# Computing the skip term of ten tiles on VectorE instead of TensorE in a state-space and gated feed-forward kernel

## The chip, the cores and the metric

The kernel runs on one core of one Trainium2 chip. The metric is the device time of one execution in microseconds. Every run named below was correct against the reference and in the fast state, with a mean granted TensorE clock of 0.996 or more of full speed in its profile. "Span" is the length of one profiled execution; it is about 1.8 us shorter than the time of the same execution.

## The reference, cut to what matters

```python
def _A_ref(x, Lambda_re, ..., Dskip):            # x: 1 x 2048 x 512
    ...                                          # h[t] = Lam_bar * h[t-1] + Bu[t]
    y = 2.0 * einsum("blp,dp->bld", hseq, Cmat).real + x * Dskip[None, None, :]
    return y

def _B_ref(x, w_gate, w_up, w_down):             # F = 1376
    return (_gelu(x @ w_gate) * (x @ w_up)) @ w_down

xn = _layernorm(x)
s = _A_ref(xn, ...)
g = _silu(_B_ref(xn, ...))
return x + s * g
```

The change concerns one term, `xn * Dskip`, an elementwise product.

## The kernel before

The 2048 rows are worked in four slabs of 512, each of four tiles of 128 rows by 512 columns. For each slab TensorE does eleven gate steps (gate and up products, four matmuls each), then the input projection of the next slab (u), then four down projections (f) of eleven products. VectorE does the recurrence: rotations by cosine and sine, a scan, rotation back, which leaves the hidden state `hst`. The y tiles of a slab are placed among the gate steps of the next slab. The skip term is four more matmuls per tile, with diagonal matrices that hold Dskip, in the same accumulation as y:

```python
Y_AT = (5, 7, 9, 10)          # gate steps of the next slab after which the y tiles stand

def y_mm(s, m, hst):
    ...
    for h in range(2):
        flush(("h", s, h))    # issue all VectorE work up to the state of this slab
    y_ps = psum.tile([P, D], FP32, name="y_ps", tag="ps")
    for j in range(2 * NPT):                       # 8 products with C
        nc.tensor.matmul(y_ps[:, :], lhsT=hst[...], rhs=C2[...], start=(j == 0), stop=False)
    for kt in range(KT):                           # 4 skip products
        nc.tensor.matmul(y_ps[:, kt * P : (kt + 1) * P], lhsT=xnT[...], rhs=diagI[:, kt, :],
                         start=False, stop=(kt == KT - 1))
    pe_takes(2 * NPT + 1)
    return y_ps

def epi(s, m, y_ps, g2):                           # end of a tile
    yg = work.tile([P, D], BF16, name="yg", tag="yg")        # two buffers each
    ot = work.tile([P, D], BF16, name="ot", tag="ot")
    def f():
        TT(out=yg[:], in0=y_ps[:, :], in1=g2[:], op=ALU.mult)
        TT(out=ot[:], in0=yg[:], in1=x_tok[:, s * M + m, :], op=ALU.add)
    dve(now() + 0.3, 0.95, f)
    nc.sync.dma_start(out=out_td[mg : mg + P, :], in_=ot[:])

def ln_out(s, m):                                  # normalised input, one slab ahead
    xn = work.tile([P, D], BF16, name="xn", tag="xn", bufs=4)
    ACT(out=xn[:], in_=x_tok[:, s * M + m, :], func=AF.Identity, ...)
    nc.sync.dma_start_transpose(out=xnT[...], in_=xn[:])
```

The order of VectorE's instructions is fixed when the kernel is built, by a small model of time. `later` queues the recurrence; `dve(ready, cost, f)` places an instruction that should be ready at a time counted in TensorE's progress, after the queued pieces that fit in before it:

```python
def drain(t, late):
    while waiting and max(clk["dve"], waiting[0][0]) + waiting[0][1] <= t + late:
        pop()                 # put the next queued piece here

def dve(ready, cost, f, late=0.8):
    drain(ready, late)
    clk["dve"] = max(clk["dve"], ready) + cost
    f()
```

On the chip nothing moves any more: an instruction whose operand is late holds up everything behind it (below, the rotation stands 1.04 us behind a late z).

Of the kernel before, what the change touches and what calls it, by code (L numbers as in the profile page):

```python
# [11 lines left out]
ALU = mybir.AluOpType  # L12
FP32 = mybir.dt.float32
BF16 = mybir.dt.bfloat16
# [5 lines left out]
def kernel(  # L20
# [17 lines left out]
    nc = tc.nc  # L38
    P = 128
    S = 2048  # L40
    D = 512
    F = 1376
    KT = D // P
    NPT = 4
    H2 = NPT // 2
    TS = 512
    NS = S // TS
# [8 lines left out]
    TT = nc.vector.tensor_tensor  # L56
# [7 lines left out]
    consts = ctx.enter_context(tc.tile_pool(name="consts", bufs=1))  # L64
    work = ctx.enter_context(tc.tile_pool(name="work", bufs=2))
# [9 lines left out]
    wd = consts.tile([P, NFT, D], BF16, name="wd")  # L75
    BT = consts.tile([P, 2, KT, D], BF16, name="BT")
    C2 = consts.tile([P, 2, NPT, D], BF16, name="C2")
    pv = consts.tile([16, P], BF16, name="pv")
    at0 = work.tile([P, NFT, TS], BF16, name="at", tag="at")
    hst0 = work.tile([P, 2, NPT, TS], BF16, name="hst", tag="hst")  # L80
# [13 lines left out]
    def load_gu(i):  # L94
        a, b = CUTS[i], CUTS[i + 1]
        nc.sync.dma_start(out=wg[:, :, a:b], in_=wg_r[:, :, a:b])  # L96
        nc.sync.dma_start(out=wu[:, :, a:b], in_=wu_r[:, :, a:b])

    def load_x(s):
        nc.sync.dma_start(out=x_tok[:, s * M : (s + 1) * M, :], in_=x_r[:, s * M : (s + 1) * M, :])  # L100
# [7 lines left out]
    load_x(1)  # L108
    load_gu(1)
    load_x(2)  # L110
    for h in range(2):
        for ri, src in enumerate((A_B_re, A_B_im)):
            for pt in (h * H2, h * H2 + 1):
                nc.sync.dma_start_transpose(
                    out=BT[:, ri, :, pt * P : (pt + 1) * P], in_=src[pt * P : (pt + 1) * P, :]
                )
    load_gu(2)


    warm = consts.tile([P, TS], BF16, name="warm")  # L120
    nc.vector.memset(warm[:], 0.0)
    halfpi = consts.tile([P, 1], FP32, name="halfpi")
    nc.vector.memset(halfpi[:], math.pi / 2)
# [182 lines left out]
        GS(out=ncre[:], in0=cre[:], scalar1=-1.0, scalar2=None, op0=ALU.mult)  # L306

    def fold_c(pt):
        tA = work.tile([P, D], FP32, name="tA", tag="tA")
        tB = work.tile([P, D], FP32, name="tB", tag="tB")  # L310
        ACT(out=tA[:], in_=CT[:, 1, pt, :], func=AF.Copy, scale=cim[:, pt : pt + 1])
        ACT(out=tB[:], in_=CT[:, 0, pt, :], func=AF.Copy, scale=cim[:, pt : pt + 1])
        dve(now() + 0.8, 0.66, lambda: STT(
            out=C2[:, 0, pt, :], in0=CT[:, 0, pt, :], scalar=cre[:, pt : pt + 1], in1=tA[:],
            op0=ALU.mult, op1=ALU.subtract,
        ))
        dve(now() + 1.6, 0.66, lambda: STT(
            out=C2[:, 1, pt, :], in0=CT[:, 1, pt, :], scalar=ncre[:, pt : pt + 1], in1=tB[:],
            op0=ALU.mult, op1=ALU.subtract,
        ))  # L320
# [6 lines left out]
    def now():  # L327
        return clk["pe"]

    def pe_takes(n, one=0.2157):  # L330
        clk["pe"] += n * one
# [6 lines left out]
    def flush(key):  # L338
        while any(w[3] == key for w in waiting):
            pop()  # L340

    def drain(t, late):
        while waiting and max(clk["dve"], waiting[0][0]) + waiting[0][1] <= t + late:
            pop()
# [5 lines that stand above are left out]
# [5 lines left out]
    ini = {}  # L355
    U_BUFS = 3
    U0_AT = (5, 7)
    Y_AT = (5, 7, 9, 10)

    def ca_wide():  # L360
        ACT(out=v4(ca[:]), in_=ch[:, :, NB : NB + NA].unsqueeze(3).to_broadcast(W4), func=AF.Copy)
# [107 lines left out]
    def down(s, m, at):  # L469
        m0 = m * P  # L470
        f_ps = psum.tile([P, D], FP32, name="f_ps", tag="ps")
        for k in range(NFT):
            fs = min(P, F - k * P)
            nc.tensor.matmul(  # L474
                f_ps[:, :], lhsT=at[:fs, k, m0 : m0 + P], rhs=wd[:fs, k, :], start=(k == 0), stop=(k == NFT - 1)
            )
        pe_takes(NFT)
        g2 = work.tile([P, D], FP32, name="g2", tag="g2", bufs=6)
        ACT(out=g2[:], in_=f_ps[:, :], func=AF.Silu)  # L479
        return g2  # L480

    def y_mm(s, m, hst):
        m0 = m * P
        mg = s * TS + m0
        for h in range(2):
            flush(("h", s, h))
        y_ps = psum.tile([P, D], FP32, name="y_ps", tag="ps")
        for j in range(2 * NPT):
            nc.tensor.matmul(  # L489
                y_ps[:, :], lhsT=hst[:, j // NPT, j % NPT, m0 : m0 + P], rhs=C2[:, j // NPT, j % NPT, :],  # L490
                start=(j == 0), stop=False,
            )
        for kt in range(KT):
            nc.tensor.matmul(  # L494
                y_ps[:, kt * P : (kt + 1) * P], lhsT=xnT[:, kt, mg : mg + P], rhs=diagI[:, kt, :],
                start=False, stop=(kt == KT - 1),
            )
        pe_takes(2 * NPT + 1)
        return y_ps

    def epi(s, m, y_ps, g2):
        mg = s * TS + m * P
        yg = work.tile([P, D], BF16, name="yg", tag="yg")
        ot = work.tile([P, D], BF16, name="ot", tag="ot")

        def f():
            TT(out=yg[:], in0=y_ps[:, :], in1=g2[:], op=ALU.mult)  # L507
            TT(out=ot[:], in0=yg[:], in1=x_tok[:, s * M + m, :], op=ALU.add)

        dve(now() + 0.3, 0.95, f)  # L510
        nc.sync.dma_start(out=out_td[mg : mg + P, :], in_=ot[:])

    def y_halves(s, m, hst, g2):
# [4 lines left out]
        for i in range(2):  # L518
            c = slice(i * D // 2, (i + 1) * D // 2)
            y_ps = psum.tile([P, D // 2], FP32, name="y_ps", tag="ps")  # L520
            for j in range(2 * NPT):
                nc.tensor.matmul(  # L522
                    y_ps[:, :], lhsT=hst[:, j // NPT, j % NPT, m0 : m0 + P], rhs=C2[:, j // NPT, j % NPT, c],
                    start=(j == 0), stop=False,
# [22 lines left out]
    def ln_small(s):  # L547
# [9 lines left out]
        nc.gpsimd.tensor_tensor(out=rs[:, s, :], in0=var, in1=mhalf[:], op=ALU.pow)  # L557
        nc.gpsimd.tensor_tensor(out=nb[:, s, :], in0=nm[:, s, :], in1=rs[:, s, :], op=ALU.mult)

    def ln_out(s, m):  # L560
        xn = work.tile([P, D], BF16, name="xn", tag="xn", bufs=4)
        ACT(out=xn[:], in_=x_tok[:, s * M + m, :], func=AF.Identity, scale=rs[:, s, m : m + 1], bias=nb[:, s, m : m + 1])  # L562
        c0 = s * TS + m * P
        nc.sync.dma_start_transpose(out=xnT[:, :, c0 : c0 + P], in_=xn[:])


    clk["pe"] = 8.1
    clk["dve"] = 10.3
    hsts, ats, g2s = {0: hst0}, {0: at0}, {}
# [10 lines left out]
    def ln_vector_small(x):  # L580
        G.tensor_scalar(out=vx[:, x, :], in0=mv[:, x, :, 1], scalar1=EPS, scalar2=None, op0=ALU.add)
        G.tensor_tensor(out=rs[:, x, :], in0=vx[:, x, :], in1=mhalf[:], op=ALU.pow)
        G.tensor_tensor(out=nb[:, x, :], in0=mv[:, x, :, 0], in1=rs[:, x, :], op=ALU.mult)
        G.tensor_scalar(out=nb[:, x, :], in0=nb[:, x, :], scalar1=-1.0, scalar2=None, op0=ALU.mult)
# [12 lines left out]
    for s in range(NS):  # L597
        for j in range(NFT):
            ffn(s, j, ats[s])
            if s == 0:  # L600
                if j == 1:
                    ca_wide()
                    coefficients()
                if j == 3:
                    ln_vector_small(2)
                if j == 8:
                    coefficients_end()
                if 3 <= j < 3 + M:
                    ln_out(1, j - 3)
                if j == 2 + M:  # L610
                    load_c(0)
                    nc.sync.dma_start(
                        out=wd[:, 0 : NFT - 1, :],
                        in_=B_w_down[0 : (NFT - 1) * P, :].rearrange("(k p) d -> p k d", p=P),
                    )
                    nc.sync.dma_start(out=wd[:FL, NFT - 1, :], in_=B_w_down[(NFT - 1) * P : F, :])
                    load_c(1)
                    load_x(3)
                if j in U0_AT:
                    chain(0, U0_AT.index(j), u_pair(0, U0_AT.index(j)), hst0)  # L620
            else:
                if s < NS - 1 and 1 <= j < 1 + M:
                    ln_out(s + 1, j - 1)
                if j in Y_AT:
                    m = Y_AT.index(j)
                    epi(s - 1, m, y_mm(s - 1, m, hsts[s - 1]), g2s[s - 1, m])
        if s < NS - 1:
            hsts[s + 1] = work.tile([P, 2, NPT, TS], BF16, name="hst", tag="hst")
            ats[s + 1] = work.tile([P, NFT, TS], BF16, name="at", tag="at")
            for h in range(2):  # L630
                chain(s + 1, h, u_pair(s + 1, h), hsts[s + 1])
            for m in range(M):
                g2s[s, m] = down(s, m, ats[s])
                if s == 0:
                    fold_c(m)
                    skip_diag(m)
                if s == 1:
                    ln_act(3, m)
            if s == 1:
                ln_small(3)  # L640
    s = NS - 1
# [38 lines left out]
```

## Time and profile before

The kernel took 186.52 us (median of 3, 186.51 to 186.91) before the prediction was made.

| of the span of 184.9 us | busy us | share |
|---|---|---|
| TensorE matmuls (PE) | 178.8 | 97% |
| VectorE (DVE) | 154.3 | 83% |
| ScalarE (ACT) | 111.9 | 61% |
| GpSimd (POOL) | 20.6 | 11% |

A share is an average over stages. To weigh this change three more views are needed. The groups by shape price one instruction. TensorE's timeline gives the distance between starts, because matmuls overlap (a product with C lasts 379 ns on average, but they start 216 ns apart), so that their durations cannot be added. VectorE's timeline tells when each slab's state is complete, to be set against the moment when TensorE asks for it. The prediction shows these lines.

### The profile page before, as it was taken

The page shows a single profiled execution, that of the slowest core. Times are in us where ns is not written, and L with a number is a line of the kernel's source. Part 1 is how long each engine was busy: PE and PEld are TensorE (multiplying, and loading weights), DVE is VectorE, ACT ScalarE, POOL GpSimd, SP SyncE. Part 2 cuts the span into 40 slices and gives each one's busy share as a digit, 9 for nine tenths or more (in the row PEclk, how much of TensorE's full clock was granted, in tenths as well). Part 3 has the DMA queues.
Part 4 walks back from the last instruction along what each step waited for, and adds up shares of the span by engine and source line. Part 5 has one row for each costly group of instructions (what it writes and reads, how often), then busy time and mean ns, then how long its engine had stood idle before and what let it go on. Part 6 is the DMA issues. An engine that isn't in the chain of part 4 may idle for free.

```text
span 184.9 us, 2493 instructions
## 1 busy us (share of the span) xinstructions
PE 178.8 (97%) x887; PEld 86.0 (46%) x903; DVE 154.3 (83%) x238; ACT 111.9 (61%) x196; POOL 20.6 (11%) x44
## 2 busy tenths in 40 slices
PE   7899999999999999999999999999999999999992
PEld 2474444544444444544444444544444444554452
DVE  4978999999999999999999999989999993332034
ACT  3199997768999745267889954347339643441210
POOL 3677503600000000000004000000000000000000
PEclk9999999999999999999999999999999999999999
DMA  5999694793001400000000420100000000010001
GB/s 144 309 361 128 102 239 100 212 245 109 0 0 28 85 32 28 28 28 0 0 4 5 80 57 2 34 28 28 0 0 0 4 0 28 28 37 25 28 28 57
DMA packets 24444, 12.26 MB, mean 66 GB/s; under 512 B 15760, under 2 KB 24432, under 8 KB 24432
## 3 DMA queue, kind: packets, MB, share of 16 engines
q1 hardware_dynamic: 24256, 12.03, 27.0%
q8 instruction: 7, 0.11, 0.3%
q10 hardware_dynamic: 176, 0.07, 0.1%
q14 instruction: 5, 0.04, 0.1%
HBM read 6.33 MB, written 2.10 MB: 46 GB/s over the span
## 4 chain that ended last, share of the span: by engine, by line
PE 93%; DMA 3%; SPq 1%; issue 1%; DVE 0%
PE up_ps L228 21%; PE f_ps L474 20%; PE g_ps L228 20%; PE u_ps L373 15%; PE y_ps L489 14%; DMA wu<-in_B_w_up_dram 3%; PE y_ps L494 2%; PE y_ps L522 1%; SPq L89 1%; SPq L96 0%; PE tp L175 0%; DVE yg L532 0%; DVE ot L533 0%; PE y_ps L528 0%
## 5 line engine op out<-in xcount | busy, mean ns | idle before, releaser
L228 PE MATMUL up_ps<-xnT,wu 128*128 128x512 bf16 (+2 forms) x181 | 45.2, 370 | 0.6 <-DMA wu<-in_B_w_up_dram 0.3
L228 PE MATMUL g_ps<-xnT,wg 128*128 128x512 bf16 (+2 forms) x179 | 44.9, 369 | 0.6 <-ACT xnT L196 0.5
L461 ACT ACTIVATE gt<-g_ps 128x512 bf16<-128x512 f32 (+1 forms) x44 | 27.1, 616 | 20.4 <-PE g_ps L228 16.9
L474 PE MATMUL f_ps<-wd,at 128*128 128x512 bf16 (+1 forms) x172 | 38.5, 379 | 0.2
L462 ACT ACTIVATE ub<-up_ps 128x512 bf16<-128x512 f32 (+1 forms) x44 | 27.3, 620 | 6.7 <-PE up_ps L228 6.4
L419 DVE TENSOR_TENSOR_SCAN Ft<-rho,it,Wt 128x512 bf16<-128x512 f32 x24 | 29.2, 1266 | 0.0
L373 PE MATMUL u_ps<-xnT,BT 128*128 128x512 bf16 x127 | 28.4, 379 | 0.1
L489 PE MATMUL y_ps<-C,hst 128*128 128x512 bf16 x117 | 28.2, 379 | 0.2
L228 PEld LDWEIGHTS <-wu 128*128 128x128 bf16 (+1 forms) x184 | 18.3, 100 | 20.2 <-DMA wu<-in_B_w_up_dram 0.6
L474 PEld LDWEIGHTS <-at 128*128 128x128 bf16 (+1 forms) x176 | 17.1, 98 | 20.6
L228 PEld LDWEIGHTS <-wg 128*128 128x128 bf16 (+1 forms) x184 | 17.9, 100 | 18.1 <-DMA wg<-in_B_w_gate_dram 0.6
L378 ACT ACTIVATE U<-u_ps 128x512 bf16<-128x512 f32 x32 | 19.0, 615 | 10.8 <-PE u_ps L373 10.7
L507 DVE TENSOR_TENSOR yg<-y_ps,g 128x512 bf16<-128x512 f32 x15 | 10.3, 685 | 14.1 <-PE y_ps L494 10.3
L479 ACT ACTIVATE g<-f_ps 128x512 f32<-128x512 f32 x16 | 9.6, 598 | 18.5 <-PE f_ps L474 18.5
L373 PEld LDWEIGHTS <-BT 128*128 128x128 bf16 x128 | 12.5, 98 | 14.6
L489 PEld LDWEIGHTS <-hst 128*128 128x128 bf16 x120 | 11.7, 98 | 13.6
L467 DVE TENSOR_TENSOR at<-gt,ub 128x1024 bf16<-128x1024 bf16 x20 | 13.6, 680 | 5.0 <-ACT ub L462 5.0
L393 DVE TENSOR_TENSOR hst<-pp,qq 128x1024 bf16<-128x1024 bf16 x16 | 10.7, 686 | 0.2
L389 DVE TENSOR_TENSOR pp<-U,cos_b 128x2048 bf16<-128x2048 bf16 x8 | 9.8, 1225 | 1.2 <-ACT U L378 0.8
L155 DVE BATCH_NORM_STATS2 st<-x_tok 128x6 f32<-128x512 bf16 x12 | 7.6, 682 | 3.6 <-DMA x_tok<-in_A_x_dram 3.6
L393 DVE TENSOR_TENSOR Wt<-pp,qq 128x1024 bf16<-128x1024 bf16 x16 | 10.3, 687 | 0.2
L562 ACT ACTIVATE xn<-x_tok,nb,rs 128x512 bf16<-128x512 bf16 x12 | 10.5, 874 | 0.0
(106 smaller groups left out, 148.6 us busy)
## 6 DMA issues: line engine op xcount, KB each, us to landing
out_dram<-ot SPq DMA_DIRECT2D x15, 128.0 KB, 1.7
x_tok<-in_A_x_dram SPq DMA_DIRECT2D x3, 512.0 KB, 5.4
wd<-in_B_w_down_dram SPq DMA_DIRECT2D x1, 1280.0 KB, 6.6
wg<-in_B_w_gate_dram SPq DMA_DIRECT2D x1, 640.0 KB
wu<-in_B_w_up_dram SPq DMA_DIRECT2D x1, 640.0 KB, 9.0
wg<-in_B_w_gate_dram SPq DMA_DIRECT2D x1, 384.0 KB, 5.2
wu<-in_B_w_up_dram SPq DMA_DIRECT2D x1, 384.0 KB
wg<-in_B_w_gate_dram SPq DMA_DIRECT2D x1, 352.0 KB, 3.6
```

What stands on the lines that cost most here:

```text
L228: nc.tensor.matmul(ps[:fs, a:b], lhsT=w[:, kt, fsl], rhs=xnT[:, kt, s * TS + a : s * TS + b], start=(kt == 0), stop=(kt == KT - 1),)
L373: nc.tensor.matmul(u_ps[:, :], lhsT=BT[:, ri, kt, pt * P : (pt + 1) * P], rhs=xnT[:, kt, cols], start=(kt == 0), stop=(kt == KT - 1),)
L378: ACT(out=U[:, ri, q, :], in_=u_ps[:, :], func=AF.Copy)
L393: return lambda: TT(out=dst()[i], in0=box["pp"][:, i, :, :], in1=box["qq"][:, 1 - i, :, :], op=op)
L419: nc.vector.tensor_tensor_scan(out=box["F"][:, ri, q, :], data0=rho[:, pt : pt + 1].to_broadcast([P, TS]), data1=box["W"][:, ri, q, :], in ...
L461: ACT(out=gt[:fs, i, :], in_=g_ps[:fs, :], func=AF.Gelu_apprx_tanh)
L462: ACT(out=ub[:fs, i, :], in_=u_ps[:fs, :], func=AF.Copy)
L467: dve(now() + lag, 0.61, lambda: TT(out=at[:, j - 1 : j + 1, :], in0=gt[:], in1=ub[:], op=ALU.mult))
L474: nc.tensor.matmul(f_ps[:, :], lhsT=at[:fs, k, m0 : m0 + P], rhs=wd[:fs, k, :], start=(k == 0), stop=(k == NFT - 1))
L489: nc.tensor.matmul(y_ps[:, :], lhsT=hst[:, j // NPT, j % NPT, m0 : m0 + P], rhs=C2[:, j // NPT, j % NPT, :], start=(j == 0), stop=False,)
L507: TT(out=yg[:], in0=y_ps[:, :], in1=g2[:], op=ALU.mult)
L562: ACT(out=xn[:], in_=x_tok[:, s * M + m, :], func=AF.Identity, scale=rs[:, s, m : m + 1], bias=nb[:, s, m : m + 1])
```

## The change

The intent is to take work off the engine that sets the end. For the four tiles of slabs 1 and 2 and the first two of slab 3, VectorE multiplies xn by Dskip (loaded once, broadcast over the partitions, as `Db`) as soon as xn is made. It keeps the product `z` in one of nine buffers until y of that tile is there, and adds it in fp32. Those tiles lose their four skip products. y of slab 1 moves to gate steps 1 to 4 of slab 2 (counted from 0), and y of slab 2 to steps 2, 4, 6 and 8 of slab 3. Room for z comes from shared scratch buffers.

```diff
+    Db = consts.tile([P, D], BF16, name="Db")
 ...
     load_x(2)
+    nc.sync.dma_start(out=Db[:], in_=A_Dskip.unsqueeze(0).to_broadcast([P, D]))
 ...
-    warm = consts.tile([P, TS], BF16, name="warm")
+    warm = work.tile([P, TS], BF16, name="warm", tag="yg")
 ...                                   # tA, tB: tag "tt", bufs=3, shared with yt; g2: bufs 6 -> 4
-    Y_AT = (5, 7, 9, 10)
+    Y_AT = {1: (5, 7, 9, 10), 2: (1, 2, 3, 4), 3: (2, 4, 6, 8)}
 ...
-                start=(j == 0), stop=False,
+                start=(j == 0), stop=((s, m) in zs and j == 2 * NPT - 1),
-        for kt in range(KT):
+        for kt in range(0 if (s, m) in zs else KT):
 ...
-        pe_takes(2 * NPT + 1)
+        pe_takes(2 * NPT + ((s, m) not in zs))
 ...
-            TT(out=yg[:], in0=y_ps[:, :], in1=g2[:], op=ALU.mult)
+            y = y_ps
+            if (s, m) in zs:
+                y = work.tile([P, D], FP32, name="yt", tag="tt", bufs=3)
+                TT(out=y[:], in0=y_ps[:, :], in1=zs[s, m][:], op=ALU.add)
+            TT(out=yg[:], in0=y[:, :], in1=g2[:], op=ALU.mult)
 ...
-        dve(now() + 0.3, 0.95, f)
+        dve(now() + 0.3, 1.6 if (s, m) in zs else 0.95, f)
 ...
+    def skip(s, m, xn):
+        zs[s, m] = work.tile([P, D], BF16, name="z", tag="z", bufs=9)
+        dve(now() + 1.5, 0.34, lambda: TT(out=zs[s, m][:], in0=xn[:], in1=Db[:], op=ALU.mult))
 ...                                   # in ln_out
+        if s < NS - 1 or m < 2:
+            skip(s, m, xn)
 ...                                   # in the main loop: y of a step now comes before ln_out
```

More of the change, by code (lines that the diff above doesn't have):

```diff
@@ L308, in fold_c @@
     def fold_c(pt):
-        tA = work.tile([P, D], FP32, name="tA", tag="tA")
-        tB = work.tile([P, D], FP32, name="tB", tag="tB")
+        tA = work.tile([P, D], FP32, name="tA", tag="tt", bufs=3)
+        tB = work.tile([P, D], FP32, name="tB", tag="tt", bufs=3)
         ACT(out=tA[:], in_=CT[:, 1, pt, :], func=AF.Copy, scale=cim[:, pt : pt + 1])
@@ L477, in down @@
         pe_takes(NFT)
-        g2 = work.tile([P, D], FP32, name="g2", tag="g2", bufs=6)
+        g2 = work.tile([P, D], FP32, name="g2", tag="g2", bufs=4)
         ACT(out=g2[:], in_=f_ps[:, :], func=AF.Silu)
@@ L558, in ln_small @@
         nc.gpsimd.tensor_tensor(out=nb[:, s, :], in0=nm[:, s, :], in1=rs[:, s, :], op=ALU.mult)
+    zs = {}
+    def skip(s, m, xn):
+        zs[s, m] = work.tile([P, D], BF16, name="z", tag="z", bufs=9)
+        dve(now() + 1.5, 0.34, lambda: TT(out=zs[s, m][:], in0=xn[:], in1=Db[:], op=ALU.mult))
     def ln_out(s, m):
@@ L621 @@
             else:
+                if j in Y_AT[s]:
+                    m = Y_AT[s].index(j)
+                    epi(s - 1, m, y_mm(s - 1, m, hsts[s - 1]), g2s[s - 1, m])
                 if s < NS - 1 and 1 <= j < 1 + M:
                     ln_out(s + 1, j - 1)
-                if j in Y_AT:
-                    m = Y_AT.index(j)
-                    epi(s - 1, m, y_mm(s - 1, m, hsts[s - 1]), g2s[s - 1, m])
         if s < NS - 1:
```

## The prediction

> **What bounds the kernel now.** I read the page first for who is busy and whose chain ended last.
>
> ```profile
> PE 178.8 (97%) x887; PEld 86.0 (46%) x903; DVE 154.3 (83%) x238; ACT 111.9 (61%) x196; POOL 20.6 (11%) x44
> ...
> PE   7899999999999999999999999999999999999992
> ...
> DVE  4978999999999999999999999989999993332034
> ...
> PE 93%; DMA 3%; SPq 1%; issue 1%; DVE 0%
> ```
>
> TensorE (PE) fills every slice after the start and carries 93% of the chain of work that ended last. VectorE (DVE) is just as full up to about slice 34 of 40 (157 us) and slack only after that. So TensorE sets the end now, but VectorE has nearly no idle time in which to take over work; what saves it is how far ahead of its deadlines it runs. The change moves work from the first to the second, so I need prices and deadlines. The prices are in the groups of instructions, shapes kept apart:
>
> ```profile
> L489 PE MATMUL y_ps<-C,hst 128*128 128x512 bf16 x117 | 28.2, 379 | 0.2
> ...
> L507 DVE TENSOR_TENSOR yg<-y_ps,g 128x512 bf16<-128x512 f32 x15 | 10.3, 685 | 14.1 <-PE y_ps L494 10.3 <-ACT g L479 3.8
> ...
> L508 DVE TENSOR_TENSOR ot<-yg,x_tok 128x512 bf16<-128x512 bf16 x15 | 6.4, 425 | 0.5
> ...
> L494 PE MATMUL y_ps<-diagI,xnT 128*128 128x128 bf16 x60 | 5.8, 219 | 0.0
> ```
>
> The matmul means of 379 and 219 ns overlap each other; what a matmul costs is the distance between starts, which the timeline of TensorE gives around the first y tile of slab 0:
>
> ```profile
> 61.27 1.89 PE L489 MATMUL y_ps<-C,hst 128*128 128x512 bf16 x8
> 63.00 0.39 PE L494 MATMUL y_ps<-diagI,xnT 128*128 128x128 bf16 x4
> 63.22 1.03 PE L228 MATMUL g_ps<-xnT,wg 128*128 128x512 bf16 x4
> ```
>
> Eight products with C take 1.73 us (216 ns each), the four skip products 63.22 - 63.00 = 0.22 us (about 56 ns each). After 9 us that timeline shows no idle entry at all. The deadlines on VectorE's side are the ends of the hidden state, in its timeline:
>
> ```profile
> 57.23 1.28 DVE L393 TENSOR_TENSOR hst<-pp,qq 128x1024 bf16<-128x1024 bf16 x2
> ...
> 150.55 0.68 DVE L393 TENSOR_TENSOR hst<-pp,qq 128x1024 bf16<-128x1024 bf16 x1
> 151.15 0.68 DVE L507 TENSOR_TENSOR yg<-y_ps,g 128x512 bf16<-128x512 f32 x1
> ```
>
> State of slab 0 is complete at 58.5 and its y begins at 61.27: 2.8 us of lead. State of slab 3 is complete at 151.2 and its y begins at 164.13: 12.9 us. For slabs 1 and 2 the same timelines give 91.1 against 104.48 and 123.3 against 147.70.
>
> **What the Trainium skill says.** "TensorE: Matmul & The Clock Gate", under "Wait — 56ns, not 53.3ns?", puts a warm matmul at N / 2.4 GHz plus about 2.5 ns, 55.6 ns for N = 128 and 215.7 ns for N = 512; the distances above (56 and 216) agree. "VectorE: DVE Perf Modes", section "The perf-mode tier table", gives tensor_tensor twice the rate for bf16 in SBUF and the single rate for fp32 or any PSUM operand; 425 against 685 ns agrees. So the product of xn and Db costs about 0.42 us, and an addition out of PSUM into fp32 about 0.69; the multiplication that follows reads two fp32 tiles in SBUF and stays at 0.69. "PSUM — Partial Sum Buffer", section "Engine vs sequencer instructions", says that the VectorE queue is strictly first in, first out and that matmuls start and complete in program order. The timelines agree in that a late operand holds up whatever stands behind it (the stop at 59.97 below). This makes the order of instructions decisive, so I compared the built instruction streams of both kernels, engine by engine.
>
> **The change part by part.**
>
> *Removed on TensorE.* Ten tiles (four of slab 1, four of slab 2, two of slab 3) lose 4 products each: 10 x 0.223 us = 2.23 us, all on the path that sets the end.
>
> *Added on VectorE.* Pitches, start to start, from its timeline: 0.34 us for a bf16 product that nothing behind it waits for (69.84 to 70.18 for ot), 0.72 for an operation out of PSUM whose result the next one reads (69.12 to 69.84). Ten products and ten additions: 10 x (0.34 + 0.72) = 10.6 us, taking VectorE from 154.3 busy to about 154.3 + 10 x (0.425 + 0.685) = 165.4, or 90% of the span. It costs the kernel nothing unless a deadline is missed, so I walk the new VectorE order and compare it with TensorE.
>
> *Deadline 1, y of slab 0 (61.27).* Ahead of the last state operation of slab 0 the new order has the four z of slab 1 (4 x 0.34 = 1.36), three z of slab 2 (1.02) and one more gate product (0.60). Worse, the second z of slab 2 stands behind an xn that ScalarE (ACT) only finishes at 58.96:
>
> ```profile
> 56.45 0.83 ACT L562 ACTIVATE xn<-x_tok,nb,rs 128x512 bf16<-128x512 bf16 x1
> ...
> 58.11 0.85 ACT L562 ACTIVATE xn<-x_tok,nb,rs 128x512 bf16<-128x512 bf16 x1
> ```
>
> The walk: first half of the back rotation at 54.29 + 1.36 = 55.65 (+0.05 for the fourth z, which just meets its xn); gate product 56.8; first z 57.4; the second would be due at 57.75 and waits until 59.0, 1.3 us of idling; second half of the rotation 59.36; first state operation 60.6; gate product 61.2; third z 61.8; last state operation 62.16 to 62.85 instead of 58.5. TensorE waits for it only at the seventh of the eight products (the built stream has that wait on its weight load), due at 61.27 + 6 x 0.2157 = 62.56. With 0.1 us for the load it starts near 63.0: **a new stop of about 0.45 us**.
>
> *Deadline 2, y of slab 1, brought forward to the second gate step of slab 2.* Due about 94.1 + 0.45 + 2 x 1.73 = 98.0. Its state moves from 91.1 to about 94.5 (7 or 8 z, the 1.3 us, less VectorE's 0.4 us of idle time there): 3.4 us to spare. Placing y early matters for buffers: z has nine, and the tenth product needs the first freed.
>
> *Deadline 3, y of slab 3.* From the last state operation of slab 0 (offset 62.16 - 57.84 = 4.32) to that of slab 3 VectorE gets three more z (1.02), seven additions (7 x 0.72 = 5.04), three more y tiles of slab 2 ahead of it because their steps move from 5, 7, 9, 10 to 2, 4, 6, 8 (3 x 1.06 = 3.18), and it loses 1.21 us of old idle time; one gate product comes in (0.60) and one was counted already (0.60). It starts at 150.55 + 4.32 + 1.02 + 5.04 + 3.18 - 1.21 = 162.9 and ends at 163.6. TensorE reaches y of slab 3 at 164.13 - 8 x 0.223 + 0.45 = 162.8 and needs the last piece at the seventh product, 164.1. It just holds. Behind it stand the last y of slab 2 (1.78), then the two last gate products, done near 166.0 and 166.4; the down projection asks for them at 162.8 + 16 x 0.2157 = 166.2 and at 166.7. That holds by 0.2 to 0.3 us, and my sum over 100 us of VectorE is no better than about 0.5 us: I charge 0.15 us on average.
>
> *Beside other work.* The load of Db takes one more slot of the sync queue (about 0.5 us, as the slots around it) and 128 KB. The weights wd are the closest thing behind it: issued at 32.7, landed 6.6 us later at 39.3, needed at 41.40. Hidden. The shared scratch of three buffers and g2 with four: each reuse is met by more than 0.5 us in the walk. In slabs 2 and 3 a PSUM bank that holds y comes round again eight tiles later; the tightest, third y of slab 2, frees at about 159.6 for a gate tile at 161. At the very end, the second tile of slab 3 now takes VectorE 1.78 us and the next arrives 1.95 us later, so the tail stays as it is.
>
> *Sum:* 186.52 - 2.23 + 0.45 + 0.15 = 184.9 us.
>
> **Rivals.** (1) *Full gain, 184.3.* Speaks for it: VectorE is off the chain (0%) and no TensorE idle time follows 9 us. Against: it counts shares and not deadlines; the lead of 2.8 us at slab 0 is less than the delay worked out. (2) *VectorE becomes the bound in slab 3.* Were it 2 us later than summed, the whole delay would fall on y of slab 3 and the down projection: about 186.5, no gain, or a loss beyond that. For: it has no idle time between about 17 and 152 us. Against: the costs are measured in this trace and old idle time is absorbed. (3) *The extra load delays the first slab*, a stop of 0.5 to 1 us near 19 us (B weights) or 41 us (wd): about 185.7. Against: wd has 2.1 us of slack in the queue. (4) *Slower by over 2%* would need some 6 us of new stops; only ScalarE held back by gate buffers that VectorE frees late would chain like that, and the walk leaves at least 4 us there.
>
> **Range and chances.** The floor is the full gain, 184.3, less a tenth for noise; the top allows about 1.2 us more in stops than I sum: 184.2 to 186.1. Faster by over 2% would need 182.8, 1.5 us below what removing the products can give: 0.01. Within 2%: 0.96. Slower: 0.03.
>
> **What would show it right or wrong.** The groups should show 20 skip products at the full-width line instead of 60, ten z near 0.42, ten yt near 0.69, and yg still near 0.69. TensorE's timeline should have one stop of 0.3 to 0.6 us inside the first y of slab 0, released by the state operation, with VectorE idle before the second z of slab 2; y of slab 1 without a wait; state of slab 3 complete near 163.6 with at most some tenths of waiting around 163 to 167. I am wrong if VectorE shows no idle time at that z, if TensorE waits over 1 us in slab 3, or if it waits on a transfer before 45 us.

## The result and the profile after

| | median us | range | runs |
|---|---|---|---|
| before | 186.66 | 186.51 to 186.91 | 4 |
| changed | 184.96 | 184.40 to 185.17 | 4 |

The ratio is 0.9903, with a 95% interval of 0.9877 to 0.9929. A ratio is the mean time of one kernel's fast runs over the mean of the other's in the same rounds, so it is not quite the ratio of the medians quoted beside it. The gain is about 1%. All outputs are right.

First the page of the changed kernel: busy shares, slices of the span, and the chain that ended last by engine and by line.

```profile
PE 177.8 (97%) x863; PEld 83.7 (46%) x863; DVE 163.5 (89%) x258; ACT 112.8 (62%) x196; POOL 19.9 (11%) x44
...
DVE  4886999999997999999999999999999999996053
...
PE 87%; DMA 4%; DVE 4%; ACT 2%; SPq 1%; issue 0%; DVEq 0%
PE f_ps L476 21%; PE up_ps L230 19%; PE g_ps L230 19%; PE u_ps L375 15%; PE y_ps L491 13%; DMA wu<-in_B_w_up_dram 3%; DMA out_dram<-ot 1%; ACT gt L463 1%; ACT ub L464 1%; ACT xn L575 1%; DVE hst L395 1%; SPq L90 1%; DVE qq L391 1%; PE y_ps L496 0%; DVE z L571 0%; DVE yg L513 0%
```

TensorE's row of slices reads exactly as before. VectorE is now full up to slice 36 instead of 33, and its busy time rose by 9.2 us. The chain is the most telling line. TensorE had 93% of it and has 87%, and a small group is new: ScalarE's gt, ub and xn, VectorE's z, qq and hst, and a store of ot. These are pieces of the two waits found below.

The groups, shapes kept apart (line, engine, operation, output and inputs, count | busy us, mean ns | idle before):

```profile
L513 DVE TENSOR_TENSOR yg<-yt,g 128x512 bf16<-128x512 f32 x10 | 6.9, 693 | 1.4 <-ACT g L481 1.0
L512 DVE TENSOR_TENSOR yt<-y_ps,z 128x512 f32<-128x512 f32 x10 | 6.8, 680 | 7.1 <-PE y_ps L491 7.1
...
L571 DVE TENSOR_TENSOR z<-xn,Db 128x512 bf16<-128x512 bf16 x10 | 4.1, 418 | 1.0 <-ACT xn L575 1.0
...
L496 PE MATMUL y_ps<-diagI,xnT 128*128 128x128 bf16 x20 | 1.9, 219 | 0.0
```

There are 20 skip products at this width instead of 60, ten additions and ten products. Only one z had to wait, for 1.04 us. TensorE's timeline (start, duration, engine, line, operation, count) shows where that went, in y of slab 0, slab 1 and slab 3:

```profile
61.43 2.21 PE L491 MATMUL y_ps<-C,hst 128*128 128x512 bf16 x8
63.47 0.39 PE L496 MATMUL y_ps<-diagI,xnT 128*128 128x128 bf16 x4
...
98.05 1.89 PE L491 MATMUL y_ps<-C,hst 128*128 128x512 bf16 x8
99.78 1.03 PE L230 MATMUL g_ps<-xnT,wg 128*128 128x512 bf16 x4
...
162.82 1.89 PE L491 MATMUL y_ps<-C,hst 128*128 128x512 bf16 x8
164.55 1.67 PE L476 MATMUL f_ps<-wd,at 128*128 128x512 bf16 x7
```

Read the distance from the start of the C products to the next entry. It is 1.73 us without a stop, as in slabs 1 and 3. In slab 0 it is 63.47 - 61.43 = 2.04 us, a stop of 0.31 us that prints no idle note, because it lies within a row. The tile of slab 1 goes straight on to a gate product.

VectorE's timeline says why, and what slab 3 looks like:

```profile
57.69 0.42 DVE L571 TENSOR_TENSOR z<-xn,Db 128x512 bf16<-128x512 bf16 x1
59.15 0.42 DVE L571 TENSOR_TENSOR z<-xn,Db 128x512 bf16<-128x512 bf16 x1 [1.04 <-ACT xn L575]
59.49 1.22 DVE L391 TENSOR_TENSOR qq<-Ft,sin_b 128x2048 bf16<-128x2048 bf16 x1
...
62.29 0.69 DVE L395 TENSOR_TENSOR hst<-pp,qq 128x1024 bf16<-128x1024 bf16 x1
...
162.11 1.29 DVE L395 TENSOR_TENSOR hst<-pp,qq 128x1024 bf16<-128x1024 bf16 x2
...
165.10 0.69 DVE L469 TENSOR_TENSOR at<-gt,ub 128x1024 bf16<-128x1024 bf16 x1
165.70 0.42 DVE L467 TENSOR_TENSOR at<-gt,ub 96x512 bf16<-96x512 bf16 x1
```

Behind the second z of slab 2 stand the second half of the rotation (qq) and the last two state operations of slab 0. The very last one, which the seventh C product needs, ends at 62.98. The seventh C product was due at 61.43 + 6 x 0.2157 = 62.72 and started two products before 63.47, at 63.04. In slab 3 the state is complete at 163.40, and the last gate products end at 165.79 and 166.12; no product waits for them.

A last difference is at the end. These are the last operations of VectorE, first before, then changed:

```profile
181.66 0.42 DVE L532 TENSOR_TENSOR yg<-y_ps,g 128x256 bf16<-128x256 f32 x1
182.12 0.29 DVE L533 TENSOR_TENSOR ot<-yg,x_tok 128x256 bf16<-128x256 bf16 x1
```

```profile
179.95 0.29 DVE L539 TENSOR_TENSOR ot<-yg,x_tok 128x256 bf16<-128x256 bf16 x1 [0.46 <-DMA out_dram<-ot]
180.16 0.42 DVE L538 TENSOR_TENSOR yg<-y_ps,g 128x256 bf16<-128x256 f32 x1
180.61 0.29 DVE L539 TENSOR_TENSOR ot<-yg,x_tok 128x256 bf16<-128x256 bf16 x1
```

TensorE's last matmul ended at 181.63 before and at 179.87 in the changed kernel. The rest took 182.41 - 181.63 = 0.78 us before and 180.90 - 179.87 = 1.03 us after, because the first half of the last tile waited for the store of the tile two before it, which still held one of the two ot buffers.

The two spans are thus accounted for:

| term | us | from |
|---|---|---|
| 40 skip products gone | -2.23 | 10 x 0.223 |
| stop in the first y of slab 0 | +0.31 | 2.04 - 1.73 |
| TensorE reaches that y later | +0.16 | 61.43 - 61.27 |
| tail | +0.25 | 1.03 - 0.78 |
| sum | -1.51 | spans: 183.4 - 184.9 = -1.5 |

The term of 0.16 us is there from the start: the first gate product began at 7.49 us before and at 7.70 here. In the seven other profiles of the changed kernel and its close variants (all below that leave GpSimd and slab 3 as they are, and the one with twelve tiles) it lies between 7.41 and 8.13 us. So I take it as scatter of the start. There is only one profile of the kernel before, so whether the change also moves the mean start stays open.

### The profile page after: what moved, and what is told of

Its sections match the earlier page's. It is cut to its first block, busy times and chain, and to the rows that moved or that the text cites. A ratio compares the mean times of both kernels' runs of the same rounds, so it can differ in the third digit from the quotient of the medians.

```text
span 183.4 us, 2452 instructions
## 1 busy us (share of the span) xinstructions
PE 177.8 (97%) x863; PEld 83.7 (46%) x863; DVE 163.5 (89%) x258; ACT 112.8 (62%) x196; POOL 19.9 (11%) x44
## 4 chain that ended last, share of the span: by engine, by line
PE 87%; DMA 4%; DVE 4%; ACT 2%; SPq 1%; issue 0%; DVEq 0%
PE f_ps L476 21%; PE up_ps L230 19%; PE g_ps L230 19%; PE u_ps L375 15%; PE y_ps L491 13%; DMA wu<-in_B_w_up_dram 3%; DMA out_dram<-ot 1%; ACT gt L463 1%; ACT ub L464 1%; ACT xn L575 1%; DVE hst L395 1%; SPq L90 1%; DVE qq L391 1%; PE y_ps L496 0%; DVE z L571 0%; DVE yg L513 0%
## 5 line engine op out<-in xcount | busy, mean ns | idle before, releaser
L230 PE MATMUL g_ps<-xnT,wg 128*128 128x512 bf16 (+2 forms) x184 | 45.6, 370 | 0.5 <-ACT xnT L198 0.5
L512 DVE TENSOR_TENSOR yt<-y_ps,z 128x512 f32<-128x512 f32 x10 | 6.8, 680 | 7.1 <-PE y_ps L491 7.1
L395 DVE TENSOR_TENSOR hst<-pp,qq 128x1024 bf16<-128x1024 bf16 x16 | 10.6, 687 | 0.2
```

What stands on the lines that cost most here:

```text
L230: nc.tensor.matmul(ps[:fs, a:b], lhsT=w[:, kt, fsl], rhs=xnT[:, kt, s * TS + a : s * TS + b], start=(kt == 0), stop=(kt == KT - 1),)
L395: return lambda: TT(out=dst()[i], in0=box["pp"][:, i, :, :], in1=box["qq"][:, 1 - i, :, :], op=op)
```

## The experiments

My theory (A) after the result: the stop at slab 0 is caused by one product placed ahead of its operand; the tail costs another quarter of a microsecond; VectorE's remaining lead in slab 3 is only a few tenths. Rivals: the stop comes from VectorE's larger load as such, the early y matters for the time, or slab 3 has more room than it seems.

All variants start from the changed kernel. Ratios are against the kernel before in the same rounds (medians of before: 186.60, 186.92 and 186.82).

| run | call | median us (range) | ratio (95%) | span |
|---|---|---|---|---|
| e1_z_ready | 1 | 184.29 (184.18 to 184.80) | 0.9882 (0.9864 to 0.9900) | 182.4 |
| e2_ot3 | 1 | 185.05 (184.66 to 185.33) | 0.9911 (0.9896 to 0.9927) | 183.3 |
| e3_both | 1 | 184.51 (184.13 to 184.66) | 0.9881 (0.9865 to 0.9898) | 182.8 |
| e5_y_old | 1 | 184.72 (184.57 to 185.06) | 0.9900 (0.9884 to 0.9915) | 183.3 |
| e4_extra3 | 2 | 185.81 (185.38 to 186.19) | 0.9941 (0.9920 to 0.9963) | 183.6 |
| e4_extra8 | 2 | 188.27 (187.68 to 190.03) | 1.0089 (1.0036 to 1.0143) | 186.9 |
| e6_pool | 2 | 190.24 (189.87 to 191.49) | 1.0197 (1.0155 to 1.0240) | 188.3 |
| e7_pool14 | 2 | 192.95 (192.77 to 193.39) | 1.0328 (1.0309 to 1.0346) | 191.2 |
| c1_changed | 3 | 184.76 (184.51 to 185.28) | 0.9899 (0.9881 to 0.9918) | 183.4 |
| c2_z_ready | 3 | 184.37 (184.23 to 184.52) | 0.9872 (0.9850 to 0.9894) | 182.6 |
| e8_twelve | 3 | 184.96 (184.39 to 186.16) | 0.9909 (0.9883 to 0.9936) | 182.6 |

### e1_z_ready: the products of slab 2 placed when their operand is there

```diff
-        dve(now() + 1.5, 0.34, lambda: TT(out=zs[s, m][:], ...))
+        dve(now() + (2.7 if s == 2 else 1.5), 0.34, lambda: TT(out=zs[s, m][:], ...))
```

No work is taken away. Only the order on VectorE changes: rotation and state may now be placed ahead of a z whose xn is late.

> Edit: the four products for slab 2 are asked for 1.2 us later, so that the second stands behind the first state operation of slab 0 instead of in front of the rotation; nothing else moves. Theory A (the stop of 0.31 us inside the first y of slab 0 comes from VectorE idling 1.04 us for xn in front of that product): the idle entry goes, the last state operation of slab 0 ends near 61.5 us instead of 62.98, the eight products of the first y take 1.73 us from start to start instead of 2.04, and the kernel gains 0.3 us against the changed kernel (about 184.7). Rival (the stop comes from the amount of work put in front of that deadline, five z and a gate product, wait or no wait): the stop stays at 0.2 us or more, no gain.

TensorE's timeline, then VectorE's:

```profile
60.93 1.89 PE L491 MATMUL y_ps<-C,hst 128*128 128x512 bf16 x8
62.65 0.39 PE L496 MATMUL y_ps<-diagI,xnT 128*128 128x128 bf16 x4
```

```profile
56.99 0.42 DVE L571 TENSOR_TENSOR z<-xn,Db 128x512 bf16<-128x512 bf16 x1
57.33 1.22 DVE L391 TENSOR_TENSOR qq<-Ft,sin_b 128x2048 bf16<-128x2048 bf16 x1
...
60.23 0.69 DVE L395 TENSOR_TENSOR hst<-pp,qq 128x1024 bf16<-128x1024 bf16 x1
60.84 0.42 DVE L571 TENSOR_TENSOR z<-xn,Db 128x512 bf16<-128x512 bf16 x1
```

The rotation now follows one z at once, the last state operation ends at 60.92 instead of 62.98, and y takes 62.65 - 60.93 = 1.72 us: the stop is gone. From the start of that y to the last matmul it is 118.13 us, against 118.44 in the changed kernel, 0.31 less, the size of the stop. So the order in which the z of slab 2 stand before the state makes the stop. VectorE's total load is the same (163.5 us busy in both), so the rival of load as such falls. But the edit did more than was expected of it: the third z, too, now stands behind the last state operation (60.84; at 61.95 it stood before it). From the start of pp to the end of that operation it is 5.66 us (55.26 to 60.92) instead of 7.03 (55.95 to 62.98). The 1.37 us between them are the wait of 1.04 and one z of 0.34. By the changed kernel's own times either alone would have sufficed, the second barely: 62.98 - 1.04 = 61.94 and 62.98 - 0.34 = 62.64, against 62.72. That the wait is the larger part is thus measured; that it alone makes the stop is argued, and no run parts the two.

### c1_changed and c2_z_ready: both again, in the same rounds

The first is the changed kernel unaltered, the second is e1_z_ready unaltered.

> The changed kernel again, unedited, as the measure for the other two runs of this call: ratio to the kernel before near 0.990 as in its first runs, and in the profile the stop inside the first y of slab 0 again, by 0.2 to 0.4 us. If the wait of the last half tile for an ot buffer is now 0.26 us as in three later profiles and not 0.46, the end of the first profile was a slow store.

> The kernel with the four products of slab 2 asked for 1.2 us later, again, beside the changed kernel in the same rounds. Theory A (the idling of VectorE in front of the second product makes the stop): 0.3 us faster than the changed kernel of this call, first y of slab 0 in 1.73 us. Rival (the gain of its first run was start-up luck): equal to the changed kernel within 0.1 us.

c1 shows the stop again (61.63 to 63.68 for the C products, 0.32 us over 1.73) and the idle time before z (1.24 us). c2 shows neither (61.09 to 62.81). The ratios differ by 0.27%, 0.5 us; the medians differ by 0.39 us. Their intervals still overlap, so the gain in time rests on this call, on e1 and on the traces together. On all of these c2 is the best version found, by about 0.4 us over the changed kernel.

### e2_ot3 and e3_both: a third ot buffer, alone and with e1

```diff
-        ot = work.tile([P, D], BF16, name="ot", tag="ot")
+        ot = work.tile([P, D], BF16, name="ot", tag="ot", bufs=3)      # in both places
```

> Edit: three buffers for the output tile ot instead of two. Theory A (the third tile of the end is written 0.3 us late because two tiles of slab 3 now take VectorE 1.8 us each, so the first half of the last tile waits 0.46 us for the store of the tile two before it): that wait goes, and from the end of the last matmul to the end of the last VectorE operation it takes about 0.8 us instead of 1.03; gain 0.25 us (about 184.7). Rival (the wait is in the shadow of TensorE, whose last half tile comes later anyway): the distance stays at 1.0 us, no gain.

> Both edits: later z of slab 2 and three ot buffers. If both theories hold and their stretches lie apart, the gains add: 0.3 + 0.25 = 0.55 us against the changed kernel (about 184.4), with TensorE never idle after 9 us. Rival: the first gain is eaten by a new stop in slab 3, where TensorE now arrives 0.3 us earlier; but VectorE gets 1.04 us there too, so theory A expects none.

The wait is gone; VectorE's end in e2:

```profile
179.24 0.42 DVE L538 TENSOR_TENSOR yg<-y_ps,g 128x256 bf16<-128x256 f32 x1
179.69 0.29 DVE L539 TENSOR_TENSOR ot<-yg,x_tok 128x256 bf16<-128x256 bf16 x1
...
180.53 0.29 DVE L539 TENSOR_TENSOR ot<-yg,x_tok 128x256 bf16<-128x256 bf16 x1
```

TensorE ends at 180.04 in this profile and VectorE at 180.82, 0.78 us later, as in the kernel before. Yet no gain shows in the time: e2's ratio is 0.9911, and e3's is the same as e1's. This part of theory A was a miss in size. In the other profiles with two buffers the wait is 0.26 to 0.39 us, not 0.46, and the tail is 0.82 (e1), 0.83 (e5), 0.89 (c1) and 0.95 (c2): 0.04 to 0.17 over the 0.78 of before. In the first profile the store was a little slower: 1.99 us from its issue (177.96) to the operation that waited (179.95), against 1.79 in e1 and 1.92 in c2.

### e5_y_old: y at the old steps

```diff
-    Y_AT = {1: (5, 7, 9, 10), 2: (1, 2, 3, 4), 3: (2, 4, 6, 8)}
+    Y_AT = {1: (5, 7, 9, 10), 2: (5, 7, 9, 10), 3: (5, 7, 9, 10)}
-        zs[s, m] = work.tile([P, D], BF16, name="z", tag="z", bufs=9)
+        zs[s, m] = work.tile([P, D], BF16, name="z", tag="z", bufs=10)
```

> Edit: y of all slabs stays at the old steps (5, 7, 9, 10) with ten z buffers; the ten tiles still lose their skip products. Theory A (the earlier steps only free z buffers and are neutral in time, since TensorE had 3.4 us of lead at y of slab 1): time within 0.2 us of the changed kernel, no TensorE stop in slab 2; in slab 3 the state is complete about 1.8 us earlier (near 161.6 us), because one y tile less stands in front of it. Rival (the move is needed: with y late VectorE's additions pile up at the end of each slab): a stop of over 0.5 us before the down projection of slab 2 or 3, slower than the changed kernel by that.

```profile
160.60 1.29 DVE L395 TENSOR_TENSOR hst<-pp,qq 128x1024 bf16<-128x1024 bf16 x2
```

The state of slab 3 is complete at 161.89 instead of 163.40, because less of y stands ahead of it on VectorE. The time is the same within the interval; slabs 2 and 3 have no stop and slab 0 keeps its own (0.32 us). The early y is neutral here: it costs 1.5 us of lead in slab 3 that TensorE does not ask for, and saves one z buffer.

### e4_extra3 and e4_extra8: useless work on VectorE in slab 3

```diff
+    scr = consts.tile([P, D], BF16, name="scr")
 ...                                   # end of gate step 2 of slab 3; 3 or 8 times
+                        TT(out=scr[:], in0=Db[:], in1=Db[:], op=ALU.mult)
```

> Edit: three useless bf16 products (0.34 us each, 1.0 us in all) on VectorE in slab 3, just before the first y tile of slab 2. Theory A (slab 3 holds by only 0.3 us, counted at the last two gate products against the down projection): TensorE stops for about 0.7 us in all around 163 to 167 us; slower than the changed kernel by about 0.7 us (185.6). Rival (VectorE has slack to give there, as a busy share of 89% suggests): no stop, same time.

> Edit: eight useless products (2.7 us) at the same place. Theory A: a stop of 2.7 - 0.3 = 2.4 us in slab 3, time about 187.4, slower than the kernel before. Rival (slack of 2 us or more): under 0.7 us.

VectorE's timeline of e4_extra3 gives the price of three:

```profile
144.94 1.34 DVE L640 TENSOR_TENSOR scr<-Db 128x512 bf16<-128x512 bf16 x3
146.19 1.22 DVE L391 TENSOR_TENSOR qq<-U,sin_b 128x2048 bf16<-128x2048 bf16 x1
```

From start to start they put off the next instruction by 146.19 - 144.94 = 1.25 us; eight put it off by 3.55 (145.91 to 149.46). TensorE's timeline of e4_extra3, then of e4_extra8:

```profile
162.38 0.59 PE L491 MATMUL y_ps<-C,hst 128*128 128x512 bf16 x2
163.69 1.47 PE L491 MATMUL y_ps<-C,hst 128*128 128x512 bf16 x5 [0.71 <-DVE hst L395]
164.99 1.24 PE L476 MATMUL f_ps<-wd,at 128*128 128x512 bf16 x5
```

```profile
163.42 1.02 PE L230 MATMUL up_ps<-xnT,wu 128*96 128x512 bf16 x4 [0.76 <-DVE yt L512]
...
166.95 1.47 PE L491 MATMUL y_ps<-C,hst 128*128 128x512 bf16 x5 [2.08 <-DVE hst L395]
```

With three, y of slab 3 takes 164.99 - 162.38 = 2.61 us instead of 1.73. A delay of 1.25 us makes a stop of 0.88, so the lead was 1.25 - 0.88 = 0.37 us. The stop is where I had not looked for it: at the third product, which needs the first of the last two state operations. In the changed kernel that operation was done at 162.11 + 0.69 = 162.80 and its product due at 162.82 + 2 x 0.2157 = 163.25: a margin of 0.45 us. In e4_extra3 the product started 0.06 us after that operation ended (163.63 to 163.69), and with this taken off the margin is 0.39. With eight, the stretch from the first y of slab 2 to the down projection of slab 3 takes 25.62 us (142.64 to 168.26) against 22.45 in the changed kernel. That is 3.17 us for 3.55 us of delay, 0.38 less: three readings of one lead of about 0.4 us. (Both stops exceed the expected 0.7 and 2.4 us, because these products were priced at 0.34 us each.) Beyond that lead VectorE's time is TensorE's time, one for one. At eight a second wait appears: a PSUM tile that the addition yt has not yet freed.

### e6_pool and e7_pool14: z on GpSimd, which is 89% idle

```diff
-        dve(now() + 1.5, 0.34, lambda: TT(out=zs[s, m][:], in0=xn[:], in1=Db[:], op=ALU.mult))
+        nc.gpsimd.tensor_tensor(out=zs[s, m][:], in0=xn[:], in1=Db[:], op=ALU.mult)
```

e7_pool14 does the same for the four tiles of slab 0 too, places the z of slab 2 after y of slab 0, and has three ot buffers.

> Edit: the ten products xn * Db on GpSimd instead of VectorE, which takes 3.4 us off VectorE. Theory A (GpSimd is idle and the two do not disturb each other): VectorE does not idle before the rotation of slab 0, the stop of 0.31 us goes, state of slab 3 complete 3 to 4 us earlier, time about 184.7. Rival, from the Trainium skill's SBUF page (a VectorE operation with two SBUF inputs and a GpSimd operation that reads SBUF block each other): VectorE operations beside each product last up to 1 us longer, VectorE loses as much as it saves, and stops stay or grow; time 185 or more.

> Edit: as e6, and slab 0 too gets its skip product that way (14 tiles, 24 skip products fewer on TensorE than before... 16 fewer than the changed kernel), products of slab 2 after y of slab 0, three ot buffers. Theory A: 16 x 0.056 = 0.9 us less on TensorE than e6 and 0.25 us at the end, time about 183.5. Rival (GpSimd blocks VectorE): stops in slab 1 and slab 3 that eat the gain, 184.5 or more.

In e6_pool, GpSimd's group and its timeline, then VectorE's timeline and TensorE's:

```profile
L571 POOL TENSOR_TENSOR z<-xn,Db 128x512 bf16<-128x512 bf16 x10 | 16.4, 1654 | 23.6 <-ACT xn L575 21.9 <-DVE yt L512 1.7
```

```profile
59.15 3.16 POOL L571 TENSOR_TENSOR z<-xn,Db 128x512 bf16<-128x512 bf16 x2 [20.45 <-ACT xn L575]
62.49 1.37 POOL L571 TENSOR_TENSOR z<-xn,Db 128x512 bf16<-128x512 bf16 x1 [0.18 <-ACT xn L575]
```

```profile
59.65 1.65 DVE L469 TENSOR_TENSOR at<-gt,ub 128x1024 bf16<-128x1024 bf16 x1
61.22 3.19 DVE L395 TENSOR_TENSOR hst<-pp,qq 128x1024 bf16<-128x1024 bf16 x2
```

```profile
62.91 1.04 PE L491 MATMUL y_ps<-C,hst 128*128 128x512 bf16 x4 [1.20 <-DVE hst L395]
64.47 0.60 PE L491 MATMUL y_ps<-C,hst 128*128 128x512 bf16 x2 [0.52 <-DVE hst L395]
```

The Trainium skill, "SBUF — State Buffer", section "Who interferes with whom", says that a VectorE instruction with two SBUF inputs contends with a GpSimd instruction that reads SBUF, and calls the ports that the two share an exclusive lock. The trace agrees. The gate product that starts at 59.65 lasts 1.65 us instead of 0.68. The first z, half of the pair, ends near 59.15 + 1.58 = 60.73, and 0.6 us later, at 61.30, the gate product ends. The two state operations take 3.19 us instead of 1.29, their last ending half a microsecond after the third z (63.86). So VectorE, ten products lighter, is busy for 169.0 us instead of 163.5, and TensorE stops for 1.20 and 0.52 us at y of slab 0. The idle engine is not free. TensorE also stops for 1.50 and 0.90 us in slab 2, on PSUM tiles held by yt, but there a second cause is mixed in: the edit takes the z out of the model that orders VectorE's work, too. The first yt of slab 1 (108.15) now stands behind four scans and a carry, where in the changed kernel (101.81) it stood behind two scans. How the loss divides between the two causes, no run tells.

e7 is worse by another 2.7 us with four more tiles off TensorE: 14 products of 1549 ns on GpSimd, and further stops, among them 1.41 us in the down projection of slab 0, 0.62 us at its y and 1.94 us in a u product. It is no clean test of four more tiles either: GpSimd itself waited 18.4 us for z buffers that yt had not yet freed, nine of them for 14 tiles. (The expectation's "24" should read 56 skip products fewer than before, 14 x 4.)

### e8_twelve: two more tiles, of slab 0

```diff
-    Y_AT = {1: (5, 7, 9, 10), 2: (1, 2, 3, 4), 3: (2, 4, 6, 8)}
+    Y_AT = {1: (5, 7, 9, 10), 2: (1, 2, 3, 4), 3: (5, 7, 10, 10)}
 ...           # z of slab 0, tiles 2 and 3, in gate steps 2 and 3; z of slab 2 in steps 6 to 9 of slab 1;
 ...           # z bufs 10; the state of slab 3 is flushed ahead of the last gate product
```

> Edit: twelve tiles (two of slab 0 as well), the products of slab 2 after the first y of slab 0, two y tiles of slab 2 moved behind the last state operation of slab 3 with the state flushed ahead of them, ten z buffers. Theory A (what counts is each deadline, and VectorE has about 2 us before y of slab 3 once the idling is gone and two y tiles stand behind): 2 x 0.223 us less on TensorE and no stop, 0.45 us faster than the kernel with the later products, about 184.0. Rival (ten tiles already use up VectorE; each further tile costs 1.06 us there and comes back as a stop in slab 3): stops of 0.5 us or more around y of slab 3, no gain or a loss.

```profile
158.22 4.05 PE L491 MATMUL y_ps<-C,hst 128*128 128x512 bf16 x18
162.70 1.47 PE L491 MATMUL y_ps<-C,hst 128*128 128x512 bf16 x5 [0.42 <-DVE hst L395]
164.00 2.32 PE L476 MATMUL f_ps<-wd,at 128*128 128x512 bf16 x10
```

The stretch holds three y tiles, which need 3 x 1.73 = 5.19 us and take 164.00 - 158.22 = 5.78: a stop of 0.59 us in slab 3 eats the 2 x 0.223 = 0.45 us of the two tiles. The stop at slab 0 is absent (61.05 to 62.78). In time it does not beat c2. (In two of its six runs the time exceeds the span by 2.4 and 3.1 us instead of 1.8, but the medians of the spans say the same: 182.95 against 182.55.) With this order of VectorE's work, ten tiles are what the lead pays for.

## Why the prediction was right or wrong

The predicted 184.9 us stands against a median of 184.96, inside the range. The main mechanism was right: 2.23 us go from TensorE's path, and one missed deadline at slab 0 gives some of it back. That the sum agrees to 0.06 us is luck. The stops were charged at 0.60 us and came to 0.31, while the tail (0.25) and a later start (0.16) were not foreseen at all, and the four runs scatter from 184.40 to 185.17.

- **Removed on TensorE (2.23 us)**: right. The tiles without skip products take 1.73 us, and 20 skip products are left.
- **Added on VectorE (10.6 us, 165.4 busy)**: right in kind, with z at 418, yt at 680 and yg at 693 ns. Busy is 163.5, so 9.2 us were added. (VectorE was full up to slice 33 before, about 152 us, not 34 and 157 us as the text first reads it; the walk used the timeline. The stop "at 59.97 below" is not among the lines shown; it is 0.19 us before a gate product.)
- **Deadline 1 (0.45 us)**: right in place and in what causes it, mis-sized by 0.14 us. The stop is 0.31 us in the first profile and 0.32 in c1 and e2. The walk put the end of the last state operation at 62.85, 0.29 us past the due time of 62.56; it ended at 62.98, 0.26 past 62.72. The product then started 0.06 us after that end, not 0.1, and the walk had rounded its restart up to 63.0. TensorE's later arrival (0.16 us) does not explain the smaller stop, since VectorE's chain, which waits for ScalarE's xn, came later with it: in c1 y began at 61.63, the state ended at 63.19, and the stop was the same. The idle time before z was 1.04 to 1.24 us, predicted 1.3. e1 shows that the order is the cause: with it changed, the stop goes.
- **Deadline 2**: right. The last pair of state operations of slab 1 ended at 94.6 (predicted 94.5), and y began at 98.05 (predicted 98.0) without a wait.
- **Deadline 3 (0.15 us)**: the walk over 100 us was good to 0.2 us, with the state complete at 163.40 (predicted 163.6). The charge was not needed: no stop in the changed kernel's two profiles. The step that named the tightest point was wrong. The last gate products (ready at 165.79 and 166.12, asked for at 162.82 + 16 x 0.2157 = 166.27 and two products later at 166.70) had 0.48 and 0.58 us; the third product of y, at which the walk did not look, had 0.45. It is close, but e4 shows that the third product stops first. e4 also measured the lead, about 0.4 us, nearer to the predicted 0.2 to 0.3 than to plenty.
- **"The tail stays as it is"**: wrong by 0.25 us in the first profile and by about 0.1 as a rule. The walk asked whether VectorE has time for each tile, but not when the ot buffer of the tile two before comes free. e2 shows that this was the wait.
- **Beside other work, the load of Db**: hidden as predicted, but the slot was mis-sized. Its issue held the sync queue for 2.10 us instead of about 0.5 (1.43 to 3.12 in the other runs). The load of wd was issued at 33.87 instead of 32.68. The profile has no landing for its 1280 KB; the last 96 KB of wd, issued behind it at 34.49, landed 6.4 us later, near 40.9. The first product with wd began at 41.55 without a wait. TensorE's only wait on a transfer is the old one of 0.3 us near 8.7 us.

Of the rivals, the full gain of 184.3 was missed by the stop and the tail; e1 (184.29) and c2 (184.37) reach it with the stop removed. VectorE as the bound in slab 3 is not what happened, but e4_extra8 shows it to be about 0.4 us away.

## What to carry to other kernels

When work moves from the bound engine to one that is off the chain, price the removed part by distances between starts, and then look for deadlines: list what now stands ahead of each result that the bound engine asks for, in the built order, and when each operand of those instructions is ready. A cheap instruction placed one operand too early can delay everything behind it; moving it and those behind it back (one constant here) recovered the 0.3 us. Before using an idle engine, ask what it shares with the busy one, and measure the lead that is left by adding useless work until the time moves.

## What the Trainium skill lacked or had wrong

- "GPSIMD Engine Reference", section "3.1 Elementwise — side-by-side cycle accounting", prices tensor_tensor for fp32 alone, at about 2.6 cycles per element and 1.96 times VectorE's time. For 128x512 in bf16 the mean here was 1654 ns beside a busy VectorE (1549 ns in e7_pool14), against 418 ns on VectorE: 4 times, in part because the two engines disturbed each other (the shortest z in e6 took 1.20 us). The page says nothing of bf16.
- "SBUF — State Buffer", section "Who interferes with whom", had the rule right but gives no cost for this pair: a VectorE product of 0.68 us lasted 1.65 us, and two operations of 1.29 us together lasted 3.19 us.
- "VectorE: DVE Perf Modes", section "The DRAIN you can't avoid", says that a semaphore after each of eight copies costs nothing extra. It gives no distance for products that all write the same tile. Here a product of 0.42 us is followed by an instruction with another output 0.34 us after its start (61.95 to 62.29), but the eight products of e4_extra8, which took 3.63 us and write one tile, start (3.63 - 0.42) / 7 = 0.46 us apart. Where the 0.12 us come from, no run tells.
- No page that I read gives the time for which a load that repeats one source row over 128 partitions holds the queue that issues it. That of Db, 128 KB, held it for 2.10 us (1.43 to 3.12 in the other runs), against 0.58 us for a slot of 1280 KB (wd) later on. The load ahead of Db in the queue held it for 2.12 us too, so part of this may be a queue that was full; no run here separates the two.
